# A planned attention and feed-forward kernel: other issue costs for SyncE, second engines only for work due soon, PE's operands taken as ready somewhat later than they end

## The chip, the cores and the metric

The kernel runs on one core of a Trainium2 chip. The core has a matmul engine (PE), a vector engine (DVE), an activation engine (ACT), a general engine (POOL, GpSimd) and SyncE (SP), which issues all DMAs of this kernel; each runs its own list of instructions in order and waits on semaphores. The metric is the time of one launch in device microseconds, the median of several runs.

## The reference

Causal attention over 4 batches, 12 heads, 448 positions and 64 columns a head, then a feed-forward layer pair with an ELU between. Weights come as float64, the rest as float32.

```python
scores = scale * np.matmul(q, k.transpose(0, 1, 3, 2))
scores = np.where(mask, -1000000000.0, scores)          # mask: above the diagonal
scores = scores - np.max(scores, axis=-1, keepdims=True)
attn = np.exp(scores)
attn = attn / (np.sum(attn, axis=-1, keepdims=True) + 1e-09)
x = np.matmul(attn, v)                                  # [B,H,S,D] -> [B*S, H*D] = [1792, 768]
h = x @ w_in                                            # 768 x 2048
g = np.where(h > 0.0, h, np.exp(np.minimum(h, 0.0)) - 1.0)
out = g @ w_out                                         # 2048 x 768
```

## The kernel before

All activations lie transposed, 128 rows of features by 448 columns. A matmul in full precision is made of three in a faster format: each operand is split into a high part (a cast, line 685 on ACT or 686 on DVE) and a low part (the difference, line 688 on DVE or POOL), and `three` (lines 727 to 729) adds high x high, high x low and low x high. Such a **triple** is the unit of PE's main work. Names: `xh`, `xl` are the parts of x, `ph`, `pl` those of a piece of the hidden layer, `whl` both parts of a weight block, `qkhl` those of a block of q and k; `hp` and `op` are the sums of the first and the second layer in PSUM, `G` and `u` hidden values, `w` a weight block.

The weights are converted from float64 on the way (lines 646 to 657: DVE, ACT, DVE, ACT and at last a sum of integers on POOL, `w<-w,w`, which only POOL can do), kept in DRAM and fetched again. In a part of the work one multiplication of blocks in eight is saved by sums and differences of blocks, and these sums (line 693, on DVE or POOL: `G<-G`, `u<-u`, `w<-w` of 384 or 256 columns) are extra work.

Attention goes beside the main matmuls. A group of scores `sc` (line 528) is followed on DVE by the masked copy with its row maximum `nm` (line 335), on ACT by the exponential (339), on PE by transposes `tr` (593), on ACT or DVE by their copy `at` (597), and on PE by the product with the values, `av` (561). Scores and transposes share four PSUM places, the ring `p`: a new tile gets a place when the last reader of the tile that held it is done.

The order of every engine's list comes from a planner, `Plan`. All work is added to it first, each piece with its ways (an engine, a cost in us, the function that writes the instruction), what it reads and writes, and a due time worked back from when PE should do its matmuls. `run` then plays the whole program in a model: of the pieces that could start earliest it takes the one with the earliest due time and writes it to its engine's list. A piece with two ways (casts: ACT, then DVE; differences and sums: DVE, then POOL) goes the second way when that ends it `LEAST` = 0.8 us sooner than waiting for the first, by the model. `port` marks pieces that the model doesn't let run on DVE and POOL at once. A piece is ready `HOP` = 0.22 us after its last operand on another engine; a place of a ring is free as long after its last reader's end (`free_at` in `run`). A load is in place when all earlier ones have been moved, plus `LANDS`.

What the chip does differs from the model where its costs do; the lists stay as they were written.

Of the kernel before, what the change touches and what calls it, by code (L numbers as in the profile page):

```python
# [11 lines left out]
U32 = mybir.dt.uint32  # L12
# [5 lines left out]
CP = 112  # L18
# [90 lines left out]
class Plan:  # L109
# [7 lines left out]

    LANDS = 3.2

    def __init__(self):  # L120
        self.works, self.cap = [], 1e9

# [27 lines left out]
    def run(self):  # L150
        for n, w in enumerate(self.works):
            w.n = n
        for w in reversed(self.works):
            cost = w.ways[0][1]
            lead = 2.0 * cost + 0.4 + (8.0 + 2.0 * w.size if w.size else 0.0)
            dues = [s.due - lead for s in w.succs]
            least = min(dues, default=1e9) - self.AHEAD
            for x in w.bufs:
                if x.ring and not x.ring.in_order:
                    if x.n + x.ring.places < len(x.ring.bufs_of):  # L160
                        dues.append(x.ring.bufs_of[x.n + x.ring.places].due - lead)
                dues += [max(o.due - lead, least if x.ring.long else -1e9) for o in x.after]
            if w.due is None:
                w.due = min([w.cap] + dues)
            for x in w.bufs:
                x.due = min(x.due, w.due)
            w.missing = len(w.preds)
        free, ported = {}, {}
        backlog = {}
        moved = 0.0  # L170
        ready = {w: 0.0 for w in self.works if not w.missing}
        todo = len(self.works)
        self.log = []
        self.done = []
        while todo:
            starts = {}
            for w, t in ready.items():
                skip = {}
                for b in w.bufs:
                    if not b.placed:  # L180
                        f = b.ring.free_at(b, skip.get(b.ring, 0))
                        skip[b.ring] = skip.get(b.ring, 0) + 1
                        if f is None:
                            t = None
                            break
                        t = max(t, f + self.HOP)
                if t is None:
                    continue
                for way, (eng, cost, _, port) in enumerate(w.ways):
                    s = max(t, free.get(eng, 0.0))  # L190
                    if port:
                        s = max([s] + [f for e, f in ported.items() if e != eng])
                    if way:
                        e0, c0 = w.ways[0][:2]
                        before = sum(
                            o.ways[0][1] for o, to in ready.items()
                            if o is not w and o.ways[0][0] == e0 and o.due < w.due and to <= s
                        )
                        if max(t, free.get(e0, 0.0)) + before + c0 < s + cost + self.LEAST:
                            continue  # L200
                    starts.setdefault(eng, []).append((s, w.due, w.n, way, w))
            assert starts, "no work can start"
            eng, cands = min(starts.items(), key=lambda kv: min(kv[1])[0])
            s0 = min(cands)[0]
            s, _, _, way, w = min((c for c in cands if c[0] <= s0 + 0.12), key=lambda c: (c[1], c[2]))
            _, cost, fn, port = w.ways[way]
            if port:
                ported[eng] = s + cost
            for b in w.bufs:
                if not b.placed:  # L210
                    b.placed = True
                    b.ring.order.append(b)
                    b()
            free[eng], w.eng = s + cost, eng
            if w.size:
                moved = max(moved, s + cost) + w.size
                w.end = moved + self.LANDS
            else:
                w.end = s + cost
            self.log.append((s, w.end, eng, w.due, cost))  # L220
            self.done.append(w)
            fn()
            del ready[w]
            todo -= 1
            for b in w.bufs:
                b.left -= 1
                b.end = max(b.end, w.end)
            for o in w.succs:
                o.missing -= 1
                if not o.missing:  # L230
                    o.ready = max(
                        p.end + (0.0 if p.eng == o.ways[0][0] and not p.size else self.HOP) for p in o.preds
                    )
                    ready[o] = o.ready

# [2 lines left out]
def attention_moe_kernel(ctx, tc, qk, v, w_in, w_out, out):  # L238
# [68 lines left out]
    def pool(n, fn, rate=2.3e-3):  # L307
        return ("POOL", 0.1 + rate * n, fn, True)

    def dma(kb, rows, fn, reads, writes, least=0.0, store=False):  # L310
        size = rows * (15.7 + 39.2 * kb / rows) / 16.0e3
        call = (lambda: fn(nc.sync)) if store else fn
        plan.add(("SP", 0.36 if rows <= 128 else 0.57, call, False), reads, writes, size=max(least, size))

# [161 lines left out]
    def loads_23(p, b):  # L478
        n = 2 * CP + S
        raw, hl, t = new("w", [P, n], name="qk"), new("w6", [P, 2, n], F32R, "qkhl"), new("v", [CP, 2, NCH, D])  # L480
        src = qk[b, 2 * p:2 * p + 2].rearrange("h d t s -> (h d) (t s)")[:, 2 * CP:]
        dma(n // 2, P, lambda: nc.sync.dma_start(out=raw(), in_=src), [], [raw])
        dma(224, CP, lambda: nc.sync.dma_start(out=t(), in_=v[b, p]), [], [t])
        hi_lo(lambda: hl()[:, 0], lambda: hl()[:, 1], raw, n, (hl, 0), (hl, 1), raw)
        done(raw)
        return [dict(
            reads=[hl], v=(t, lambda half, x: t()[:, half, x]), split=((0, 0), (0, 1), (1, 0)),
            q=lambda d, i, g=g: hl()[d, i, chunk(g)], k=lambda d, i, n: hl()[d, i, 2 * CP:2 * CP + n],
        ) for g in range(2)]
# [140 lines left out]
    def load64(key):  # L630
        r = words[key] = new("w6", [P, KT, P, 2], U32, "w64")
        if key[0] == "i":
            n, out, src = KT, lambda: r().rearrange("p k c w -> p k (c w)"), w_in[key[1]]
        else:
            x, n = key[2], 4
            out = lambda: r()[:, :n].rearrange("p (h k) c w -> p h k (c w)", h=2)
            src = w_out[key[1]].rearrange("p (h f) c -> p h f c", h=2)[:, :, 2 * x:2 * x + 2]
        dma(n * P, P, lambda: nc.sync.dma_start(out=out(), in_=src.bitcast(U32)), [], [r])

    def convert(key):  # L640
        r, w = words.pop(key), new("w", [P, KT, P])
        n = KT if key[0] == "i" else 4
        size = n * P
        low, high = (lambda: r()[:, :n, :, 0]), (lambda: r()[:, :n, :, 1])
        wf = lambda: w()[:, :n]
        plan.add(dve(size, lambda: nc.vector.tensor_scalar(
            wf(), f32(high()), MOST, -MOST, op0=ALU.min, op1=ALU.max
        ), 0.55e-3, 0.06, True), [(r, 1)], [w])

        plan.add(act(size, lambda: nc.scalar.activation(wf(), wf(), AF.Prelu, scale=REBIAS, alpha=2.0 ** 32), 0.09), [], [w])  # L650
        plan.add(dve(size, lambda: nc.vector.tensor_scalar(  # L651
            wf().bitcast(U32), wf().bitcast(U32), 3, None, op0=ALU.logical_shift_left
        ), 0.55e-3, 0.06, True), [], [w])
        plan.add(act(size, lambda: nc.scalar.activation(
            low().bitcast(I32), low(), AF.Copy, scale=2.0 ** -29
        ), 0.16), [], [(r, 0)])
        plan.add(pool(size, lambda: nc.gpsimd.tensor_tensor(  # L657
            out=wf().bitcast(I32), in0=wf().bitcast(I32), in1=low().bitcast(I32), op=ALU.add
        )), [(r, 0)], [w])
        if key[0] == "i":  # L660
            done(r)
            home, src = kin[key[1]], wf
        else:
            h = key[1] // HALF_E
            home = kout[key[1]].rearrange("p (h f) c -> p h f c", h=2)[:, h:, 2 * key[2]:2 * key[2] + 2]
            src = lambda: wf().rearrange("p (h f) c -> p h f c", h=2)[:, h:]
        k = kept[key] = Buf(None, lambda: home)
        dma(n * 64, P, lambda eng: eng.dma_start(out=home, in_=src()), [w], [k], store=True)
        return w if key[0] == "i" else (w, r)

    def fetch(f):
# [168 lines left out]

    def raw_piece(srcs, reads, dst):
        w = new("w", [P, KT, P])
        dma(KT * 64, 2 * P, lambda: nc.sync.dma_start(out=dst(w()), in_=srcs), reads, [w])
        return in_two(w, KT)

    GROUPS = ((1, 2), (6, 7, 4), (5, 3))
# [265 lines left out]
```

## Time and profile before

| | |
|---|---|
| time, median of 3 runs | 625.55 us (623.75 to 629.59) |
| the profiled execution | 623.13 us, span 621.4 us |
| mean granted clock of PE in it | 0.997 |
| busy of the span | PE 97%, DVE 82%, ACT 69%, POOL 26% |
| chain that ended last, by engine | PE 56%, DVE 15%, ACT 10%, DMA 9%, issue 6% |

The span is the time from the first to the last instruction in one profiled execution; the time of that execution lies 1.7 us above it, and 2.4 us below the median of the runs. Busy time of PE is counted from the start to the end of each matmul, and matmuls overlap, so a busy PE isn't PE at its peak. The chain is followed back from the last instruction to whatever released each one.

### The profile page before, as it was taken

How to read it: one execution, taken by the hardware profiler on the slowest of the kernel's cores; microseconds unless marked ns; L12 is line 12 of the kernel's file. 1: busy time of each engine (PE TensorE's matmuls, PEld its weight loads, DVE VectorE, ACT ScalarE, POOL GpSimd, SP SyncE). 2: the span in 40 equal slices, each digit the busy share in tenths (PEclk: the TensorE clock that was granted, in tenths of full speed). 3: DMA queues.
4: the chain of work that ended last, by engine and by line, in shares of the span. 5: the costliest groups of instructions: out<-in, count | busy, mean ns of one | idle time of the engine just before them, and what ended most of it. 6: DMA issues, size and time to landing. Idle time of an engine off the chain costs nothing.

```text
span 621.4 us, 11699 instructions
## 1 busy us (share of the span) xinstructions
PE 600.4 (97%) x4056; PEld 514.9 (83%) x4056; DVE 508.5 (82%) x1126; ACT 425.9 (69%) x960; POOL 163.2 (26%) x116
## 2 busy tenths in 40 slices
PE   5999999998999999999999999999999999999997
PEld 5655688877788888788788878999999889999996
DVE  4897788689998998989998798597678999998611
ACT  6988889878899989786688684365446765573300
POOL 0235532144343445242220610030001352010000
PEclk9999999998999999999999999999999999999999
DMA  9999999877999999888868598864332343352111
GB/s 218 292 355 360 386 287 271 230 224 247 297 342 344 372 308 300 282 266 261 260 214 268 195 291 243 240 171 127 107 116 84 101 126 104 104 151 69 39 51 45
DMA packets 114172, 135.95 MB, mean 219 GB/s; under 512 B 42560, under 2 KB 86848, under 8 KB 114112
## 3 DMA queue, kind: packets, MB, share of 16 engines
q1 hardware_dynamic: 114112, 135.20, 71.2%
q8 instruction: 32, 0.52, 0.4%
q14 instruction: 28, 0.23, 0.1%
HBM read 103.02 MB, written 32.15 MB: 218 GB/s over the span
## 4 chain that ended last, share of the span: by engine, by line
PE 56%; DVE 15%; ACT 10%; DMA 9%; issue 6%; POOL 2%; SPq 1%; POOLq 0%; DVEq 0%; ACTq 0%
PE op L727 9%; PE op L728 8%; PE op L729 8%; PE hp L727 6%; PE hp L729 5%; PE hp L728 5%; PE hp L749 5%; ACT a L339 4%; PE av L561 3%; PE sc L528 3%; DMA R<-rdram 3%; DMA w<-in_w_out 2%; DVE whl L688 2%; DVE a L335 2%; PE tr L593 2%
## 5 line engine op out<-in xcount | busy, mean ns | idle before, releaser
L685 ACT ACTIVATE whl<-w 128x768 fp32r<-128x768 f32 x90 | 75.6, 842 | 76.8 <-PE op L729 41.4
L727 PE MATMUL op<-ph,whl 128*128 128x448 f32 x336 | 126.6, 377 | 0.0
L728 PE MATMUL op<-pl,whl 128*128 128x448 f32 x336 | 122.8, 365 | 0.0
L729 PE MATMUL op<-ph,whl 128*128 128x448 f32 x336 | 122.7, 365 | 0.0
L688 DVE TENSOR_TENSOR whl<-w,whl 128x768 fp32r<-128x768 f32 x102 | 105.1, 1031 | 20.1 <-ACT whl L685 19.4
L339 ACT ACTIVATE a<-a,nm 112x448 f32<-112x448 f32 (+3 forms) x192 | 97.7, 520 | 28.4 <-DVE nm L335 27.9
L657 POOL TENSOR_TENSOR w<-w,w 128x512 int32<-128x512 int32 (+1 forms) x40 | 67.2, 1683 | 134.7 <-DVE w L651 76.5
L335 DVE CUSTOM_DVE_ANT_0 a<-sc,mask 112x448 f32<-112x448 f32 (+3 forms) x192 | 74.0, 442 | 11.9 <-PE sc L429 7.9
L727 PEld LDWEIGHTS op<-ph,whl 128*128 128x128 f32 x336 | 63.2, 188 | 8.6 <-issue 3.8
L729 PEld LDWEIGHTS op<-ph,whl 128*128 128x128 f32 x336 | 63.1, 188 | 5.1
L728 PEld LDWEIGHTS op<-pl,whl 128*128 128x128 f32 x336 | 63.3, 188 | 4.3
L727 PE MATMUL hp<-ph,whl 128*128 128x448 f32 x168 | 61.7, 367 | 1.4 <-DVE u L815 1.3
L729 PE MATMUL hp<-ph,whl 128*128 128x448 f32 x168 | 61.4, 365 | 0.0
L728 PE MATMUL hp<-pl,whl 128*128 128x448 f32 x168 | 61.3, 365 | 0.0
L597 ACT ACTIVATE at<-tr 112x448 f32<-112x448 f32 (+1 forms) x120 | 53.1, 496 | 5.9 <-PE tr L593 5.9
L727 PE MATMUL hp<-xh,whl 128*128 128x448 f32 x144 | 57.0, 396 | 0.0
L593 PE MATMUL tr<-ident,a 112*112 112x112 f32 x432 | 52.2, 262 | 4.3 <-DVE nm L335 4.3
L593 PEld LDWEIGHTS tr<-ident,a 112*112 112x112 f32 x432 | 45.8, 134 | 12.1 <-DVE nm L335 6.2
L729 PE MATMUL hp<-xh,whl 128*128 128x448 f32 x144 | 53.4, 371 | 0.9 <-DVE whl L688 0.8
L728 PE MATMUL hp<-xl,whl 128*128 128x448 f32 x144 | 53.1, 369 | 0.8 <-DVE xl L688 0.8
L561 PEld LDWEIGHTS av<-at,v 112*64 112x64 f32 x864 | 43.0, 137 | 12.1 <-ACT at L597 5.7
L561 PE MATMUL av<-at,v 112*64 112x112 f32 x864 | 50.9, 264 | 1.1 <-ACT at L597 0.8
(111 smaller groups left out, 1102.2 us busy)
## 6 DMA issues: line engine op xcount, KB each, us to landing
w<-kin SPq DMA_DIRECT2D x44, 384.0 KB, 5.8
w<-in_w_in SPq DMA_DIRECT2D x16, 768.0 KB, 8.3
w<-in_w_out SPq DMA_DIRECT2D x24, 512.0 KB, 6.7
w<-sout SPq DMA_DIRECT2D x32, 384.0 KB, 3.6
w<-kout SPq DMA_DIRECT2D x24, 384.0 KB, 4.5
qk<-in_qk SPq DMA_DIRECT2D x24, 336.0 KB, 5.9
kin<-w SPq DMA_DIRECT2D x16, 384.0 KB, 7.9
sout<-w SPq DMA_DIRECT2D x12, 512.0 KB, 6.9
```

The source lines that it names most:

```text
L335: plan.add(dve(n, lambda: nc.vector.tensor_tensor_reduce(out=a()[:, c], in0=sc()[:, c], in1=mask[:, S - n:], op0=ALU.add, op1=ALU.min, sca ...
L339: plan.add(act(n, lambda: nc.scalar.activation(a()[:, c], a()[:, c], AF.Exp, bias=nm()[:, x:x + 1], scale=-1.0, accum_out=su()[:, x:x + 1] ...
L561: nc.tensor.matmul(av()[half_of(half), chunk(u % 4)], o["v"][1](half, i), at()[:, chunk(x)], start=i == 0, stop=i == chunks(u) - 1,)
L593: nc.tensor.transpose(tr()[:, chunk(x)], a[:, chunk(i)], ident)
L597: act(w, lambda: nc.scalar.activation(at()[:, :w], tr()[:, :w], AF.Copy)),
L657: plan.add(pool(size, lambda: nc.gpsimd.tensor_tensor(out=wf().bitcast(I32), in0=wf().bitcast(I32), in1=low().bitcast(I32), op=ALU.add)), ...
L685: act(n, lambda: nc.scalar.activation(h(), x(), AF.Copy), 0.09),
L688: sub = lambda eng: lambda: eng.tensor_tensor(out=l(), in0=x(), in1=f32(h()), op=ALU.subtract)
L727: nc.tensor.matmul(acc(), wh(k), xh(), start=first, stop=False, skip_group_check=more)
L728: nc.tensor.matmul(acc(), wh(k), xl(), start=False, stop=False, skip_group_check=more)
L729: nc.tensor.matmul(acc(), wl(k), xh(), start=False, stop=last, skip_group_check=more)
L749: pe(ONE, lambda: nc.tensor.matmul(hp(), w[0]()[:, k], x(), start=k == 0, stop=k == KT - 1), [*w, x], [hp], due)
```

## The change

Three rules of the planner are altered; no piece of work is added or removed. A second engine isn't considered for a piece that is due over 20 us after it could start there. A piece of PE counts as ready 0.8 us later than before after its last operand (`START` = 0 lets this hold for all of them); the rule for a ring's places stays. An issue of SyncE costs 0.48 us in the model, or 0.66 for an address with more levels (`long`), instead of 0.36 and 0.57 by the number of rows.

```diff
@@ class Plan @@
     LANDS = 3.2
+
+    SOON = 20.0
+
+    SLACK, START = 0.8, 0.0
@@ Plan.run @@
                     if port:
                         s = max([s] + [f for e, f in ported.items() if e != eng])
+                    if way and w.due > s + self.SOON:
+                        continue
                     if way:
                         e0, c0 = w.ways[0][:2]
...
                     o.ready = max(
-                        p.end + (0.0 if p.eng == o.ways[0][0] and not p.size else self.HOP) for p in o.preds
+                        p.end + (0.0 if p.eng == o.ways[0][0] and not p.size else self.HOP + self.SLACK * (o.ways[0][0] == "PE" and o.due > self.START))
+                        for p in o.preds
                     )
@@ dma and its callers @@
-    def dma(kb, rows, fn, reads, writes, least=0.0, store=False):
+    def dma(kb, rows, fn, reads, writes, least=0.0, store=False, long=None):
         size = rows * (15.7 + 39.2 * kb / rows) / 16.0e3
         call = (lambda: fn(nc.sync)) if store else fn
-        plan.add(("SP", 0.36 if rows <= 128 else 0.57, call, False), reads, writes, size=max(least, size))
+        plan.add(("SP", 0.66 if (rows > P if long is None else long) else 0.48, call, False), reads, writes, size=max(least, size))
...
# long=True: v in loads_23; long=key[0] == "o": load64's load and convert's store; long=False: raw_piece
```

The lists that come out hold the same work. POOL's falls from 64 instructions of lines 688 and 693 to 7, and DVE's casts (line 686) from 45 to 2. The first list is POOL's, around the end of the first attention stage and the start of the second (`w_...<-w_...,w64_...` is the integer sum of a conversion, `pl` and `qkhl` are low parts). Before:

```order
L657 TENSOR_TENSOR w_1552<-w_1552,w64_1377 128x512
L657 TENSOR_TENSOR w_1679<-w_1679,w64_1588 128x512
L688 TENSOR_TENSOR pl_1765<-G_741,ph_1730 128x448
L688 TENSOR_TENSOR pl_1780<-G_745,ph_1756 128x448
L688 TENSOR_TENSOR qkhl_1820<-qk_1708,qkhl_1820 128x672
L657 TENSOR_TENSOR w_1879<-w_1879,w64_1769 128x512
L688 TENSOR_TENSOR pl_1978<-G_757,ph_1888 128x448
L688 TENSOR_TENSOR pl_1993<-G_782,ph_1911 128x448
L657 TENSOR_TENSOR w_1868<-w_1868,w64_1521 128x512
```

and now:

```order
L664 TENSOR_TENSOR w_1678<-w_1678,w64_1563 128x512
L700 TENSOR_TENSOR w64_1563<-w_1401,w64_1563 128x256
L664 TENSOR_TENSOR w_1569<-w_1569,w64_1407 128x512
L695 TENSOR_TENSOR xl_1828<-xs_1787,xh_1815 128x448
L664 TENSOR_TENSOR w_1855<-w_1855,w64_1772 128x512
L664 TENSOR_TENSOR w_1865<-w_1865,w64_1595 128x512
L664 TENSOR_TENSOR w_1970<-w_1970,w64_1825 128x512
```

The `pl` are gone from it, and so is all but one of the `qkhl` in the rest of the list; after its last integer sum POOL has one more instruction, where it had 49.

The second is DVE's, before the softmax of the third group of scores of the second attention stage (ISA is the masked copy with the row maximum). Before:

```order
L686 CAST ph_1911<-G_782 128x448
L822 SCALAR_TENSOR_TENSOR G_1950<-m_1831,hp_1704 128x448
L688 TENSOR_TENSOR whl_1953<-w_1488,whl_1953 128x768
L693 TENSOR_TENSOR w64_1769<-w_1879 128x256
L693 TENSOR_TENSOR w64_1769<-w64_1769,w_1552 128x256
L693 TENSOR_TENSOR w64_1769<-w_1552,w_1879 128x256
L693 TENSOR_TENSOR w64_1769<-w_1552,w64_1769 128x256
L335 ISA a_1918,nm_1920<-sc_1914,mask_71 112x336
```

and now:

```order
L695 TENSOR_TENSOR pl_1888<-G_729,ph_1753 128x448
L700 TENSOR_TENSOR w64_1772<-w_1855 128x256
L700 TENSOR_TENSOR w64_1772<-w64_1772,w_1569 128x256
L700 TENSOR_TENSOR w64_1772<-w_1569,w_1855 128x256
L700 TENSOR_TENSOR w64_1772<-w_1569,w64_1772 128x256
L695 TENSOR_TENSOR whl_1905<-w_1524,whl_1905 128x768
L829 SCALAR_TENSOR_TENSOR G_1967<-m_1833,hp_1695 128x448
L653 TENSOR_SCALAR w_1970<-w64_1825 128x512
L658 TENSOR_SCALAR w_1865<-w_1865 128x512
L695 TENSOR_TENSOR qkhl_1918<-qk_1780,qkhl_1918 128x672
L342 ISA a_1925,nm_1927<-sc_1921,mask_71 112x336
```

The cast has gone to ACT, and DVE makes the `pl` and the `qkhl` itself.

The third is PE's, late in the second attention stage, from a group's last transposes to its values. Before, two triples stand between:

```order
L593 MATMUL tr_4996<-ident_66,a_4753 112x112 x4
L727 MATMUL op_4928<-ph_4722,whl_4658 128x448
L728 MATMUL op_4928<-pl_4729,whl_4658 128x448
L729 MATMUL op_4928<-ph_4722,whl_4658 128x448
L727 MATMUL op_4944<-ph_4699,whl_4658 128x448
L728 MATMUL op_4944<-pl_4720,whl_4658 128x448
L729 MATMUL op_4944<-ph_4699,whl_4658 128x448
L561 MATMUL av_4876<-at_4990,v_4373 64x112
```

and now four, of which the last row and the values behind it are left off here:

```order
L600 MATMUL tr_4987<-ident_66,a_4753 112x112 x4
L734 MATMUL op_4870<-ph_4732,whl_4660 128x448
L735 MATMUL op_4870<-pl_4742,whl_4660 128x448
L736 MATMUL op_4870<-ph_4732,whl_4660 128x448
L734 MATMUL op_4885<-ph_4716,whl_4660 128x448
L735 MATMUL op_4885<-pl_4723,whl_4660 128x448
L736 MATMUL op_4885<-ph_4716,whl_4660 128x448
L734 MATMUL op_4885<-ph_4732,whl_4660 128x448
L735 MATMUL op_4885<-pl_4742,whl_4660 128x448
L736 MATMUL op_4885<-ph_4732,whl_4660 128x448
L734 MATMUL op_4953<-ph_4716,whl_4660 128x448
L735 MATMUL op_4953<-pl_4723,whl_4660 128x448
```

The values moved back by two triples. Between a group's scores and the transposes that follow them stood five or six triples in 19 of 23 groups of this stage and three or four in the others; now there are three to five in 21 of them and six in two.

## Rows read from the trace of the kernel before

**Rows 1.** The page: busy us (share of the span) and number of instructions

```profile
PE 600.4 (97%) x4056; PEld 514.9 (83%) x4056; DVE 508.5 (82%) x1126; ACT 425.9 (69%) x960; POOL 163.2 (26%) x116
```

**Rows 2.** Busy time by stretch: length, each engine (instructions), granted clock, DMA share, GB/s

```profile
404.00:466.00 62.00, 62.00 (x308) 57.48 (x307) 48.05 (x76) 31.33 (x53) 5.77 (x3) 1.00 0.45 130
```

**Rows 3.** Waits of PE: us in total, times, longest us

```profile
PE sc L429 <- DMA k<-in_qk: 5.4, 2, 4.5
PE tr L593 <- DVE nm L335: 4.3, 4, 2.2
...
PE hp L727 <- DVE u L815: 1.3, 1, 1.3
PE hp L728 <- DVE xl L688: 0.8, 1, 0.8
PE av L561 <- ACT at L597: 0.8, 1, 0.8
PE hp L729 <- DVE whl L688: 0.8, 1, 0.8
```

**Rows 4.** Waits of PE's weight loads, the same columns

```profile
PEld av L561 <- ACT at L597: 5.7, 17, 1.0
```

**Rows 5.** Timeline of PE: start us, us, instruction [idle before <- releaser]

```profile
147.55 0.37 PE L729 MATMUL hp<-xh,whl 128*128 128x448 f32 x1
150.15 0.93 PE L593 MATMUL tr<-ident,a 112*112 112x112 f32 x6 [2.24 <-DVE nm L335]
```

**Rows 6.** Timeline of DVE before that transpose

```profile
145.87 1.38 DVE L688 TENSOR_TENSOR whl<-w,whl 128x768 fp32r<-128x768 f32 x1
147.17 1.37 DVE L693 TENSOR_TENSOR w<-w 128x256 f32<-128x256 f32 x1
...
148.91 0.42 DVE L693 TENSOR_TENSOR w<-w 128x256 f32<-128x256 f32 x1
...
149.59 0.50 DVE L335 CUSTOM_DVE_ANT_0 a<-sc,mask 112x336 f32<-112x336 f32 x1
```

**Rows 7.** Timeline of POOL in the same microseconds

```profile
145.13 3.13 POOL L688 TENSOR_TENSOR pl<-G,ph 128x448 fp32r<-128x448 f32 x2
```

**Rows 8.** Timeline of DVE, and of POOL, from 249 us

```profile
249.40 2.06 DVE L688 TENSOR_TENSOR pl<-G,ph 128x448 fp32r<-128x448 f32 x1
251.38 1.50 DVE L693 TENSOR_TENSOR w<-w 128x384 f32<-128x384 f32 x1
...
254.78 0.96 DVE L688 TENSOR_TENSOR whl<-w,whl 128x768 fp32r<-128x768 f32 x1
...
249.02 1.96 POOL L688 TENSOR_TENSOR qkhl<-qk,qkhl 128x672 fp32r<-128x672 f32 x1
250.94 1.52 POOL L693 TENSOR_TENSOR G<-G 128x448 f32<-128x448 f32 x1
```

**Rows 9.** Groups by form: count | busy us, mean ns | idle before, releasers

```profile
L688 DVE TENSOR_TENSOR whl<-w,whl 128x768 fp32r<-128x768 f32 x102 | 105.1, 1031 | 20.1 <-ACT whl L685 19.4
L688 DVE TENSOR_TENSOR pl<-G,ph 128x448 fp32r<-128x448 f32 x54 | 34.9, 662 | 0.6 <-ACT ph L685 0.4
L693 DVE TENSOR_TENSOR w<-w 128x384 f32<-128x384 f32 x25 | 19.1, 765 | 1.9 <-DMA w<-kin 1.4
L686 DVE CAST whl<-w 128x768 fp32r<-128x768 f32 x18 | 10.7, 595 | 7.5 <-PE hp L729 5.4 <-POOL w L657 1.7 <-PE op L729 0.4
...
L685 ACT ACTIVATE whl<-w 128x768 fp32r<-128x768 f32 x90 | 75.6, 842 | 76.8 <-PE op L729 41.4 <-PE hp L729 15.9 <-issue 8.7
```

**Rows 10.** Busy time of two stretches, columns as in 2

```profile
150.00:156.00 6.00, 5.85 (x29) 4.99 (x31) 6.00 (x15) 5.10 (x14) 2.74 (x2) 0.72 0.93 283
124.00:373.00 249.00, 241.91 (x1917) 206.00 (x1916) 229.15 (x515) 203.35 (x474) 92.69 (x63) 0.99 0.88 280
```

**Rows 11.** The page's groups: the integer sums on POOL, columns as in 9

```profile
L657 POOL TENSOR_TENSOR w<-w,w 128x512 int32<-128x512 int32 (+1 forms) x40 | 67.2, 1683 | 134.7 <-DVE w L651 76.5
```

**Rows 12.** Timeline of SyncE's queue

```profile
104.86 1.35 SPq L401 DMA_DIRECT2D R<-rdram  x2
```

More of the change, by code (lines that the diff above doesn't have):

```diff
@@ L482, in loads_23 @@
         dma(n // 2, P, lambda: nc.sync.dma_start(out=raw(), in_=src), [], [raw])
-        dma(224, CP, lambda: nc.sync.dma_start(out=t(), in_=v[b, p]), [], [t])
+        dma(224, CP, lambda: nc.sync.dma_start(out=t(), in_=v[b, p]), [], [t], long=True)
         hi_lo(lambda: hl()[:, 0], lambda: hl()[:, 1], raw, n, (hl, 0), (hl, 1), raw)
@@ L637, in load64 @@
             src = w_out[key[1]].rearrange("p (h f) c -> p h f c", h=2)[:, :, 2 * x:2 * x + 2]
-        dma(n * P, P, lambda: nc.sync.dma_start(out=out(), in_=src.bitcast(U32)), [], [r])
+        dma(n * P, P, lambda: nc.sync.dma_start(out=out(), in_=src.bitcast(U32)), [], [r], long=key[0] == "o")
     def convert(key):
@@ L667, in convert @@
         k = kept[key] = Buf(None, lambda: home)
-        dma(n * 64, P, lambda eng: eng.dma_start(out=home, in_=src()), [w], [k], store=True)
+        dma(n * 64, P, lambda eng: eng.dma_start(out=home, in_=src()), [w], [k], store=True, long=key[0] == "o")
         return w if key[0] == "i" else (w, r)
@@ L842, in raw_piece @@
         w = new("w", [P, KT, P])
-        dma(KT * 64, 2 * P, lambda: nc.sync.dma_start(out=dst(w()), in_=srcs), reads, [w])
+        dma(KT * 64, 2 * P, lambda: nc.sync.dma_start(out=dst(w()), in_=srcs), reads, [w], long=False)
         return in_two(w, KT)
```

## The prediction

> **What bounds the kernel now.** I read the page's busy times first [rows 1]. PE is busy 600.4 of the span's 621.4 us, so any gain has to come out of the 21 us in which it isn't, or out of matmuls that run slower than they need. DVE (82%) and ACT (69%) follow; POOL has 163 us. What one triple of matmuls costs is read where nothing disturbs PE: 308 matmuls in 62 us, 0.201 us each, 0.61 us a triple [rows 2].
>
> Next the waits of PE [rows 3]. The largest, 5.4 us on the first loads of `k`, no plan can shorten by much. Then 4.3 us in four waits of the transposes `tr` for `nm`, the softmax's row maximum on DVE; then single waits for `u` (1.3), `xl` (0.8), `at` (0.8) and `whl` (0.8). The weight loads of PE show the same wait of the values `av` for `at` more often: 17 times, 5.7 us [rows 4], part of it under the matmul still running.
>
> Then why DVE comes late. A transpose's output takes a place of the ring `p`, and those places are held by scores until DVE has read them, so the first row maximum of a group frees the transposes. At 147.55 PE starts a last matmul; the transposes behind it start at 150.15, after 2.24 us of idling that DVE's `nm` ended [rows 5]. In those microseconds DVE ran a `whl` of 1.38 us and a 128x256 `w` of 1.37 us, where the same `w` without company takes 0.42, and only at 149.59 the row maximum [rows 6]. Beside them POOL had two `pl` of 3.13 us together [rows 7]: both are work that the planner had given to POOL as a second engine. It is the same at 249.40, where `pl` takes 2.06 us on DVE and the 128x384 `w` after it 1.50, beside a `qkhl` and a `G` of POOL [rows 8], against means of 0.66 and 0.77 [rows 9]. So an instruction on DVE that meets one on POOL is held up by about a microsecond, and PE pays when a softmax stands behind it.
>
> The Trainium skill says why (SBUF — State Buffer, "SBUF: two separate sides"): the two engines share a pair of ports under an exclusive lock, and a DVE instruction with two SBUF inputs that meets a POOL instruction waits for all of it. The rows agree: the 1.37 us are 0.95 more than 0.42.
>
> The 2.24 us of idling have an aftermath: over 150 to 156 us the granted clock is 0.72 [rows 10], that is 2.4 GHz with a stretch at 1.2 in it. It costs 0.28 x 6 = 1.7 us.
>
> **The change, part by part.** *Second engines only for work due within 20 us.* POOL's list falls from 64 optional instructions to 7; its 40 compulsory ones (`w<-w,w`, 67.2 us [rows 11]) stay. Of the 163 us, 67 are compulsory and some 2 set up constants, so 94 us are optional. DVE receives 57 instructions: 17 `pl` and 24 sums of 448 columns at the mean of `pl`, 0.66, make 27.1 us; 6 `whl` 6.2; 5 `qkhl` at about 0.9, 4.5; 7 sums of 128x384 at 0.77, 5.4; two of 256 columns go the other way, -0.8 [rows 6, 9]. Together 42. DVE gives to ACT 17 casts of `whl` at 0.60 (10.1) and, by their columns, 6 of `qkhl` (3) and 20 of 448 columns (7): 20. Net +22 us for DVE, before any stretch is taken off. ACT takes the 17 at 0.84 (14.3) and the other 26 by their columns (14): 28 us [rows 9].
>
> What of the stretch goes? At 145.87 to 148.5 two DVE instructions lost 0.35 (1.38 against the mean of 1.03) and 0.95, in 3.13 us of POOL: 42%. Of 94 optional us that would be 39 us for the run, the upper end; the lower end is what one group shows by itself, 102 `whl` at a mean of 1.03 against 0.96 undisturbed [rows 8, 9], 7 us. I take about 25, towards the upper end, because the local rows show the collision itself. DVE's total then hardly moves (508 + 22 - 25); what moves is when it is late.
>
> That matters most from 124 to 373 us, where softmax, weights and main matmuls run together: DVE is busy 229 of 249 us, PE idles 7.1 [rows 10]. POOL has 92.7 there; less 21 compulsory ones at 1.68 (35), 57 are optional, 61% of all. DVE so takes up 26 us there, gives up about 8 of casts (40% of 20, the stage's share of the span), and loses between 4 (61% of 7) and 24 (0.42 x 57) of stretch; with 16 it stands at 231.
>
> The four long waits of `tr` should shrink from 4.3 to about 1.0, because at the two whose DVE rows I show an optional instruction of POOL stood beside the lateness: **-3.3** (bounds 0 and -4.3). With the 2.24 us goes the clock's fall: **-1.7** (0 to -1.7). The waits for `u`, `xl` and `whl` (2.9 us together) have DVE as their last engine too, but compulsory POOL work collides as before: half, **-1.5** (0 to -2.9).
>
> *PE's operands taken 0.8 us later than they end.* The planner now puts four triples between the last transposes and the values, where it put two or three: 0.6 to 1.2 us more for the copies `at`. The mean of the 17 waits is 0.34, so the step covers it. PE's own row gives 0.8, its weight loads' 5.7; I take **-2.0**, nearer to the first, since most of a weight load's wait lies under a matmul. This part moves triples about and adds none, so in return the triples between scores and transposes fall from mostly five or six to three to five. The added 0.8 us doesn't guard that place: the freeing of a ring's place is reckoned without it.
>
> *SyncE's issues at 0.48 and 0.66 us* instead of 0.36 and 0.57. In the trace two issues of `R` take 1.35 us, 0.68 each [rows 12], so the new figure is nearer for this form. No wait of PE for a DMA stands in the list except the first, and the first loads stand in the same order: **0** (-1 to +2; a later load of `w` would show first in ACT's and DVE's waits).
>
> New waits: ACT gains 28 us on 426, and the copies `at` are its work; it is at 203 of 249 in the long stage [rows 10]. I set **+1.0** (0 to +5, the size of the present waits for `at`).
>
> Sum: -3.3 - 1.7 - 1.5 - 2.0 + 0 + 1.0 = -7.5 us. The profiled execution took 623.13 us (span 621.4), so 615.6 for its like. The median of the three runs is 625.55, 2.4 above it; against that median the forecast is **618.0 us**. 1% of this kernel is 6.3 us, about what a measurement can tell from no change: the lines are 619.3 and 631.8.
>
> **Rivals.** *DVE becomes the bound and hands the gain back.* In the long stage it takes 26 us and gives up 8: 229 + 18 = 247 of 249 if no stretch vanishes, 243 at the low end of 4. Then every row maximum comes late by whatever has piled up, and the waits for `nm` stay, with fewer but longer collisions against POOL's compulsory work. For it: DVE was full in some stretches already, 6.00 of 6 us from 150 [rows 10]. Against it: the stretch is plain in the rows, and a planner that knows DVE to be busier moves sums with late due times to after 373. Gains left: the values' 2.0 and little else, less ACT's 1.0: 622 to 628, about 624.5.
>
> The Trainium skill has a rule that backs this rival (Perfetto Trace Analysis, "Optimizing Scalar/DVE Operations"): when DVE is saturated, handing some work to ScalarE or even GPSIMD may make sense. The same paragraph warns that the shared port can undo it, which is what the timelines show [rows 6 to 8]; by the rule alone the time would be this rival's 624.5.
>
> *Slower: transposes asked for too early.* With one or two triples fewer behind the scores, DVE has to free the ring's places 0.6 to 1.2 us sooner. At the four places where it was late already (4.3 us in all) each wait grows by that: +2.4 to +4.9; a wait as long as the one of 2.24 costs a fall of the clock at three more of them, 3 x 1.7 = 5.1. With about +7 the time is 632.5. It decides if DVE reaches its row maxima no sooner after the scores than before.
>
> *The change hardly touches what counts:* it does what it says by the order, but waits only change their place, and the time stays at 625.5. I count this with the first rival.
>
> **How the numbers follow.** The forecast gets 0.62, DVE as the bound (with the waits that only move) 0.26, the slower one 0.12. Forecast's own range: with all its terms at their best ends but the values' (-2.0) and no new waits, -4.3 - 1.7 - 2.9 - 2.0 = -10.9, and another -3.7 if the values' waits go in full: 611; at the other end half of the sum, 622. The range takes in the first rival, to 628, and leaves the slower one out: 611 to 628. Of the forecast's 0.62 about 0.52 lie under 619.3; the rest and the first rival are within 1%: 0.36; slower by over 1% is the third: 0.12.
>
> **What would show it.** Right: PE's waits for `nm` under 1.5 us in all, no fall of the granted clock after the start; POOL near 75 us busy; the means of DVE's `whl` and 128x384 `w` down to about 0.96 and 0.6; waits of `av` for `at` a third of 5.7; DVE near 500, ACT near 455. The first rival: DVE over 240 of the 249 us of the long stage, `nm` waits as large as now. The slower one: more than four waits of `tr` for `nm`, each beginning after only three or four triples, and falls of the clock. The forecast would be wrong altogether if PE's idle time lay in waits that the old plan didn't have, on ACT's `at` or on loads.

## The result, and the profile after

The changed kernel took 614.61 us in the median of four runs (613.98 to 619.22), the kernel before 625.83 beside it (623.75 to 629.59): a ratio of 0.9843, with an interval of 0.98 to 0.9886. The profiled execution took 614.32 us where that of before took 623.13, so 8.8 us less; the sum had 7.5.

The page of the changed kernel: span, busy times with shares and numbers of instructions, and the engines in the chain that ended last.

```profile
span 612.5 us, 11705 instructions
...
PE 598.9 (98%) x4056; PEld 513.6 (84%) x4056; DVE 493.1 (81%) x1141; ACT 451.3 (74%) x1002; POOL 76.2 (12%) x59
...
PE 75%; DMA 8%; ACT 7%; DVE 7%; SPq 2%; issue 1%; DVEq 0%; ACTq 0%
```

DVE has 15 instructions more than before and yet 15.4 us less of busy time [rows 1]; its share of the chain has gone from 15% to 7%, and PE's from 56 to 75%. Next the waits of PE and the one of its weight loads for `at` in the changed kernel (us in total, times, longest):

```profile
PE sc L436 <- DMA k<-in_qk: 5.3, 3, 4.5
PE tr L600 <- DVE nm L342: 1.6, 2, 0.9
PE hp L736 <- DVE whl L695: 1.0, 1, 1.0
PE hp L756 <- POOL w L664: 0.9, 1, 0.9
PE tr L600 <- DVE G L829: 0.3, 1, 0.3
...
PEld av L568 <- ACT at L604: 2.8, 9, 0.3
```

This is the whole list of PE. Against [rows 3, 4]: `nm` 4.3 to 1.6, `u` and `xl` gone, `at` gone from PE and halved at the weight loads; `whl` goes from 0.8 to 1.0, and POOL's `w` from 0.2 to 0.9. The windows (length, each engine with its instructions, granted clock, DMA share, GB/s):

```profile
150.00:156.00 6.00, 6.00 (x57) 4.98 (x56) 5.85 (x13) 5.69 (x11) 2.73 (x2) 1.00 1.04 306
124.00:373.00 249.00, 246.03 (x2009) 212.11 (x2010) 232.11 (x549) 216.40 (x499) 39.40 (x28) 1.00 0.92 289
404.00:466.00 62.00, 62.00 (x302) 56.31 (x301) 41.73 (x62) 37.18 (x64) 0.00 (x0) 1.00 0.35 105
```

The clock is whole where it was 0.72, PE does 57 matmuls there instead of 29, and in the same 249 us 92 more [rows 10]. The third row holds something that nobody had asked for: in 62 us without a wait the changed kernel does 302 matmuls, the one before 308 [rows 2]. The end of the document comes back to it.

The groups by form in the changed kernel (count, busy us, mean ns, idle before):

```profile
L695 DVE TENSOR_TENSOR whl<-w,whl 128x768 fp32r<-128x768 f32 x108 | 105.2, 974 | 21.7 <-ACT whl L692 19.8
L695 DVE TENSOR_TENSOR pl<-G,ph 128x448 fp32r<-128x448 f32 x64 | 39.6, 636 | 1.8 <-ACT ph L692 1.8
L700 DVE TENSOR_TENSOR w<-w 128x384 f32<-128x384 f32 x32 | 17.7, 553 | 2.5 <-DMA w<-kin 2.0
```

The timeline of DVE, and of POOL in the last line, at the softmax that answers to [rows 5 to 7]:

```profile
142.33 0.95 DVE L695 TENSOR_TENSOR whl<-w,whl 128x768 fp32r<-128x768 f32 x1
...
144.40 0.85 DVE L695 TENSOR_TENSOR qkhl<-qk,qkhl 128x672 fp32r<-128x672 f32 x1
145.17 0.50 DVE L342 CUSTOM_DVE_ANT_0 a<-sc,mask 112x336 f32<-112x336 f32 x1
...
144.56 1.86 POOL L664 TENSOR_TENSOR w<-w,w 128x512 int32<-128x512 int32 x1 [3.74 <-DVE w L658]
```

DVE's `whl` ahead of this softmax takes 0.95 us where the one of before took 1.38. POOL is idle beside it; its next instruction, beside the `qkhl` and the row maximum, is a compulsory sum. DVE has 64 `pl` of `G` now instead of 54, each 26 ns shorter in the mean. Of the three forms shown, the 384-column sums fall most, from 765 ns to 553 [rows 9].

### The profile page after: what moved, and what is told of

It reads as the page before. It is cut to its first block, busy times and chain, and to the rows that moved or that the text cites. A ratio compares the mean times of both kernels' runs of the same rounds, so it can differ in the third digit from the quotient of the medians.

```text
span 612.5 us, 11705 instructions
## 1 busy us (share of the span) xinstructions
PE 598.9 (98%) x4056; PEld 513.6 (84%) x4056; DVE 493.1 (81%) x1141; ACT 451.3 (74%) x1002; POOL 76.2 (12%) x59
## 4 chain that ended last, share of the span: by engine, by line
PE 75%; DMA 8%; ACT 7%; DVE 7%; SPq 2%; issue 1%; DVEq 0%; ACTq 0%
PE op L734 11%; PE op L735 11%; PE op L736 11%; PE hp L734 7%; PE hp L735 7%; PE hp L736 7%; PE hp L756 6%; PE av L568 5%; PE tr L600 4%; PE sc L535 4%; ACT a L346 2%; DMA sout<-w 2%; DVE a L342 2%; ACT at L604 1%; DMA w<-kin 1%; DMA w<-in_w_in 1%
## 5 line engine op out<-in xcount | busy, mean ns | idle before, releaser
L692 ACT ACTIVATE whl<-w 128x768 fp32r<-128x768 f32 x107 | 90.1, 843 | 65.6 <-PE op L736 40.5
L600 PE MATMUL tr<-ident,a 112*112 112x112 f32 x432 | 50.9, 260 | 2.0 <-DVE nm L342 1.6
L568 PE MATMUL av<-at,v 112*64 112x112 f32 x864 | 48.3, 263 | 0.0
```

Of the source, the lines that this page charges most:

```text
L568: nc.tensor.matmul(av()[half_of(half), chunk(u % 4)], o["v"][1](half, i), at()[:, chunk(x)], start=i == 0, stop=i == chunks(u) - 1,)
L600: nc.tensor.transpose(tr()[:, chunk(x)], a[:, chunk(i)], ident)
L692: act(n, lambda: nc.scalar.activation(h(), x(), AF.Copy), 0.09),
```

## Experiments

All ratios are to the kernel before, run on the same chip. Diffs are against the changed kernel; SyncE's old costs are written "SP old":

```diff
-plan.add(("SP", 0.66 if (rows > P if long is None else long) else 0.48, call, False), ...
+plan.add(("SP", 0.36 if rows <= 128 else 0.57, call, False), ...
```

### Each part alone, and each left out

| kernel | rule for second engines | later readiness | SyncE's new costs | median us | ratio [interval] |
|---|---|---|---|---|---|
| e1_soon | yes | no | no | 618.05 | 0.9885 [0.9847, 0.9923] |
| e2_slack | no | yes | no | 627.9 | 1.0039 [1.0013, 1.0065] |
| e3_sp | no | no | yes | 629.27 | 1.0078 [1.0049, 1.0107] |
| e4_again | yes | yes | yes | 617.83 | 0.987 [0.9839, 0.9901] |
| e5_no_soon | no | yes | yes | 624.77 | 0.9991 [0.9962, 1.0019] |
| e6_no_slack | yes | no | yes | 619.81 | 0.9919 [0.9893, 0.9946] |
| e7_no_sp | yes | yes | no | 617.32 | 0.9867 [0.983, 0.9904] |

**e1_soon**, the rule alone: `SLACK = 0.0`, SP old. 

> The kernel before with the rule on second engines alone (work due over 20 us later stays on its first engine). Theory A (POOL's optional work holds up DVE, and DVE's late row maxima stop PE): most of the gain is here, 617 to 620 us against 625.8, waits of the transposes for the row maximum from 4.3 to under 2 us, no fall of the granted clock after the start, the waits of the values for their copies still near 5 us on the weight loads. Rival B (the later readiness of PE's operands brings the gain): 623 to 627. Rival C (every new plan scatters by some us and this one was lucky): anything from 620 to 632, with waits at other places.

618.05 us: 1.15% faster by itself. POOL falls to 76.7 us busy, DVE to 499.5. No wait for `nm` is left in PE's list; waits for `whl` stand there instead (3.5 us in five). Against the expectation, the granted clock does fall once (0.72 from 184 to 190 us), and the weight loads wait 3.6 us for `at`, not near 5.

**e2_slack**, the later readiness alone: `SOON = 1e9`, SP old. 

> The kernel before with PE's operands taken as ready 0.8 us later, and nothing else. Theory A: the values' waits for their copies fall from 5.7 us on the weight loads to under 3, the waits of the transposes for the row maximum stay at 3 to 6 us since the ring's places aren't guarded: 622 to 625 us. Rival B: 614 to 618. Rival C: 620 to 632.

Slower by 0.4%, where theory A had a small gain. The waits of its PE:

```profile
PE tr L600 <- DVE nm L342: 3.7, 2, 2.1
PE sc L535 <- DVE nm L342: 1.8, 1, 1.8
...
PE hp L734 <- DVE nm L342: 1.5, 1, 1.5
...
PE op L734 <- DVE nm L342: 0.6, 1, 0.6
```

7.6 us for `nm`, where there were 4.3. One of them in the timeline of PE, and then of DVE and of POOL:

```profile
164.50 0.74 PE L600 MATMUL tr<-ident,a 112*112 112x112 f32 x6
166.76 1.14 PE L600 MATMUL tr<-ident,a 112*112 112x112 f32 x8 [1.53 <-DVE nm L342]
```

```profile
163.36 2.80 DVE L700 TENSOR_TENSOR G<-G 128x448 f32<-128x448 f32 x2
166.08 0.61 DVE L342 CUSTOM_DVE_ANT_0 a<-sc,mask 112x448 f32<-112x448 f32 x1
...
162.99 1.63 POOL L664 TENSOR_TENSOR w<-w,w 128x512 int32<-128x512 int32 x1 [0.37 <-DVE w L658]
164.57 2.17 POOL L700 TENSOR_TENSOR w<-w 128x256 f32<-128x256 f32 x2
```

The transposes are asked for while DVE still has two sums of 2.80 us in all, stretched beside POOL, ahead of the next row maximum; POOL's work there is first a compulsory sum, then optional ones. The waits for `at` shrink as this part was meant to do: 1.6 us at the weight loads, in six.

**e3_sp**, SyncE's costs alone: `SLACK = 0.0`, `SOON = 1e9`. 

> The kernel before with the new issue costs of SyncE alone. Theory A: no gain of its own, 623 to 628 us, waits of PE of the same size and kind as before. Rival C: the plan is drawn anew and the time moves by 3 us or more either way although no wait of PE for a load has gone.

Slower by 0.8%, with no wait of PE for a load beyond the first. What grows are waits for `whl` (4.2 us in four) and for `at` (7.8 at the weight loads, 21 times). There are only 0.3 us of waits for `nm`, although POOL has 149.9 us of work, so lateness can come out at `whl` and `at` instead. The time is above theory A's range; it is what rival C had said of a plan drawn anew. No run here tells how the other costs lead to that.

**e4_again**, the changed kernel once more, to see how far two measurements of one program lie apart. 

> The changed kernel once more, unaltered. In its trace the matmuls of the last 235 us start every 206.7 ns, in that of the kernel before every 202.7 ns, without any wait: 4 ns x 1150 matmuls = 4.6 us. If the step is fixed by the program, it is 206.7 again and the time 614 to 615. If it is drawn in each execution, some executions show 202.7 and take about 610 us, or the times fall into two groups 4 to 5 us apart.

No edit. 617.83 us, 3.2 above the first, in ratio 0.3 points; the step between matmuls is 206.7 ns again. So the program fixes the step, but not the time to within the 1 us that was expected with it.

**e5_no_soon**: `SOON = 1e9`. 

> The changed kernel without the rule on second engines (later readiness and SyncE's costs stay). Theory A, as the first runs leave it: POOL's optional work is back, and with it DVE's late row maxima, now met by transposes that stand a triple closer behind the scores: 626 to 632 us, waits of tr for nm of 3 us or more, falls of the granted clock. Rival C (plans scatter whatever the rule): 616 to 632 with no pattern.

The gain is gone, and no more than that: 624.77 us is below theory A's 626 to 632. POOL has 157.2 us again, PE waits 3.4 us for `nm`, 3.3 and 2.7 for `whl`, and the clock is at 0.72 in two windows of 6 us, from 166 and from 230.

**e6_no_slack**: `SLACK = 0.0`. 

> The changed kernel without the later readiness of PE's operands (rule on second engines and SyncE's costs stay). In the run with the rule alone, waits of the triples for whl (3.5 us in five waits, and 1.6 us for ACT's part of it) had come up. Theory A: those stay here, and the waits of the values return to 5 us or more on the weight loads: 618 to 622 us. Rival D (with POOL's optional work gone the 0.8 us have nothing left to cover): 613 to 617.

619.81 us. Waits for `whl` come up (2.8 us on DVE, 2.8 on ACT), and the clock falls twice in the long stage of 124 to 373 us (0.78 from 148 to 154, 0.72 from 228 to 234). The values' waits don't return to 5 us: 3.0 at the weight loads. Beside the two measurements of the whole change that is 0.5 and 0.8 points, and the intervals touch or nearly do.

**e7_no_sp**: SP old. 

> The changed kernel with SyncE's old issue costs. Theory A (the issue costs bring nothing): 613 to 619 us, the same waits as in the changed kernel. Rival E (truer arrival times are needed for the other two to work): 619 to 624, with waits of PE, ACT or DVE for loads.

617.32 us, the whole change's result within its interval: no worth of SyncE's costs shows in this company.

These comparisons hold a term that none of the three parts aims at. After its attention e7_no_sp, like e1_soon, e6_no_slack and e9_pool below, starts its matmuls 4 ns closer together than the changed kernel does (202.7 against 206.7 ns, see the end of the document): over some 1,140 matmuls 4.6 us, or 0.7%. What later readiness and SyncE's costs are worth beside the rule, without this, the table doesn't say. For the rule itself it does: of ten new plans (three of them below), the six with the rule for POOL lie at 0.9843 to 0.9976, the four without it at 0.9991 to 1.0181. Rival C's scatter is real, 1 to 2 points within either group, but the groups don't overlap; e8_place and e5_no_soon lie next to each other.

### The rule for second engines, cut in two

**e9_pool** and **e10_casts**, both with `SLACK = 0.0` and SP old:

```diff
-if way and w.due > s + self.SOON:
+if way and eng == "POOL" and w.due > s + self.SOON:    # e9_pool
+if way and eng != "POOL" and w.due > s + self.SOON:    # e10_casts
```

> The kernel before, with the due-time rule for GpSimd alone: a piece that is not due soon may still go to VectorE as a second engine, but not to GpSimd. Theory A (the gain of the rule is GpSimd's optional work, which stretches VectorE's own): as the rule alone, 617 to 621 us, GpSimd near 75 us busy, VectorE's w<-w,w and pl<-w at their shortest means. Theory B (the gain is VectorE's casts taken back by ScalarE): as before, 623 to 628 us, with GpSimd's work gone and nothing gained.

> The kernel before, with the due-time rule for VectorE as a second engine alone: the early casts go back to ScalarE, GpSimd keeps its optional work. Theory A (GpSimd's optional work is the cost): 623 to 628 us, GpSimd near 150 us busy, VectorE's mean for whl still above 1.02 us. Theory B (VectorE's casts are the cost): 617 to 621 us, waits of TensorE for nm and av gone although GpSimd is as busy as before.

e9_pool took 616.94 us, 0.9876 [0.9849, 0.9904], the gain of the whole rule (e1_soon); e10_casts 635.07, 1.0181 [1.0112, 1.025], so 1.8% slower than the kernel before. The busy times of e9_pool and its windows:

```profile
PE 596.7 (97%) x4056; PEld 514.5 (83%) x4056; DVE 515.1 (84%) x1180; ACT 432.3 (70%) x965; POOL 76.4 (12%) x57
```

```profile
124.00:373.00 249.00, 243.34 (x1972) 208.50 (x1970) 236.87 (x561) 209.49 (x483) 40.09 (x27) 1.00 0.91 286
```

And the busy times, waits and windows of e10_casts:

```profile
PE 612.1 (96%) x4056; PEld 520.8 (81%) x4056; DVE 498.4 (78%) x1082; ACT 451.5 (71%) x1001; POOL 159.4 (25%) x119
```

```profile
PE tr L600 <- DVE nm L342: 6.0, 5, 2.0
...
PEld av L568 <- ACT at L604: 7.4, 22, 1.0
```

```profile
124.00:373.00 249.00, 239.13 (x1871) 201.49 (x1871) 220.20 (x478) 203.36 (x469) 91.28 (x66) 0.98 0.86 269
150.00:156.00 6.00, 4.69 (x41) 3.51 (x38) 5.88 (x14) 5.51 (x11) 2.68 (x3) 1.00 0.64 224
```

Theory A holds: the rule works through POOL. How much of it is DVE's lengthening and how much POOL's own longer pieces (a `pl` of `G` took 1.61 us there in the kernel before, 0.66 on DVE) wasn't tried apart; PE waited for POOL itself only 0.2 us. Of the means that were expected to fall, the 384-column sums' is 552 ns, but that of the 256-column `w<-w,w` stays at 464 ns (457 before). The two kernels also part DVE's load from its lateness. DVE is busier in e9_pool than in any other run here, 515.1 us, and that kernel gains 1.2%; in e10_casts it has 498.4, and the transposes wait 6.0 us for `nm`, more than in any other. What theory A didn't give is the loss of 10 us in e10_casts. Its profiled execution, the longest of four, lost some 10 of its 639.4 us by a mean granted clock of 0.984, against 1.7 us by 0.997 before; its casts ahead of the copies `at` on ACT go with the 22 waits for `at`, but that the casts cause the waits wasn't tried.

### The ring's places

**e8_place** puts the readiness rule's 0.8 us on the freeing of a ring's place as well, for PE's pieces:

```diff
-t = max(t, f + self.HOP)
+t = max(t, f + self.HOP + self.SLACK * (w.ways[0][0] == "PE"))
```

> The changed kernel, and a place of a PSUM ring counts for PE as free 0.8 us later too. Theory A: the remaining waits of the transposes for the row maximum (1.6 us) go, since the plan now leaves 0.8 us behind DVE's reading: 611 to 616 us. Rival: the scores and transposes get their places later, attention is drawn out in the plan, and the time is 616 to 622.

623.58 us, 0.9976 [0.9958, 0.9994]: the expectation was wrong, nearly all of the gain is lost. The wait for `nm` does go (0.6 us), but others come up (POOL's `w` 2.1, `G` 1.9, `xl` 1.2), and the clock falls again, to 0.72 from 142 to 148 us. The rule delays every piece of PE with a ring's place, sums of the main matmuls too, and POOL is given 14 optional pieces instead of 7. What of the two costs the 6 to 9 us (against the two measurements of the changed kernel) isn't told apart.

### The rhythm of the matmuls

**nudge64** puts one matmul of 64 columns ahead of one triple in the last long run of triples (at 400 us), into the sum that this triple then overwrites; the rest of PE's list stays.

```diff
+if (i, r, k) == (1, 0, 0):
+    nc.tensor.matmul(acc()[:, :64], w[1](k), x[0]()[:, :64], start=True, stop=True)
 three(acc, w, k, x, first, last, i in (2, 3))
```

> The changed kernel with one more matmul of 64 columns ahead of the first triple of the second joint block (its sum is overwritten by the triple that follows, so nothing else changes). If the rhythm of the long run of triples is set by where the run starts against some clock of the chip, the run may fall into 202.7 ns in place of 206.7: then 610 to 613 us (some 1100 matmuls by 4 ns less). If the rhythm is set by something else in the program, or by chance of the start: 206.7 ns again and 614 to 618 us, as the changed kernel.

The timeline of PE around it:

```profile
399.62 0.37 PE L734 MATMUL op<-ph,whl 128*128 128x448 f32 x1
399.83 0.37 PE L735 MATMUL op<-pl,whl 128*128 128x448 f32 x1
400.04 0.37 PE L736 MATMUL op<-ph,whl 128*128 128x448 f32 x1
400.24 0.19 PE L931 MATMUL hp<-ph,whl 128*128 128x64 f32 x1
400.27 0.44 PE L734 MATMUL hp<-ph,whl 128*128 128x448 f32 x1
400.55 0.36 PE L735 MATMUL hp<-pl,whl 128*128 128x448 f32 x1
400.75 0.36 PE L736 MATMUL hp<-ph,whl 128*128 128x448 f32 x1
400.95 0.37 PE L734 MATMUL hp<-ph,whl 128*128 128x448 f32 x1
```

Up to the extra matmul the starts lie 206 or 207 ns apart, behind it 202.7 in the mean, to the end of the kernel. The profiled execution took 610.87 us, 3.5 less than that of the changed kernel; some 1,030 matmuls by 4 ns would be 4.1. The median of four runs, 614.38 (ratio 0.9863 [0.9804, 0.9922]), doesn't show it.

**nudge64_again**, the same kernel. 

> The kernel with the extra 64-column matmul, unaltered, a second time. If the rhythm is fixed by the program: 202.7 ns again in the whole run of triples after the last av, a profiled time of 610 to 613 us where the clock does not fall, and a median at or a little below the changed kernel's 614.6. If it is chance at each start: 206.7 ns is as likely, and the median tells nothing from the changed kernel's.

The rhythm falls at the same matmul again, at 408.66 us this time, from 206.7 to 202.7. The median of six runs is 615.96, 0.9839 [0.9801, 0.9876]: against the changed kernel still no difference that can be measured. The runs go from 611.87 to 619.31 us, and the profiled one, the longest, has 4.0 us of waits for `nm` and a clock of 0.997 in it. So what the extra matmul gives in each execution is smaller than what single waits do from one execution to the next.

## Why the prediction was right

618.0 was forecast and 614.6 measured (617.8 the second time), inside the range, and the mechanism is the one named. That the sum of -7.5 came so near the 8.8 us of the profiled execution is in part luck: two terms that it didn't have nearly cancel, as is shown below. Of its signs, the waits for `nm` (1.6 us where under 1.5 was asked) and those for `at` (half of 5.7 where a third was) were missed, the first narrowly. By its steps:

- *Transposes waiting for `nm`, -3.3:* 4.3 to 1.6, so -2.7. e1_soon has no such wait, e5_no_soon has 3.4 us of it, e9_pool none at the transposes and e10_casts 6.0: it is POOL's optional work. (e3_sp, with 0.3 us, shows that not every plan with that work has the wait.)
- *The clock, -1.7:* no fall in the profiled execution until PE has done its last matmul.
- *`u`, `xl`, `whl`, -1.5:* 2.9 to 1.0, so -1.9.
- *Values, -2.0:* 0.8 to nothing at PE, 5.7 to 2.8 at its weight loads. The part that was meant for this isn't needed for the most of it: without the later readiness the weight loads wait 3.0 (e6_no_slack) and with the rule alone 3.6. Where later readiness does show is the first attention stage, which the prediction didn't look at: PE waits 1.3 to 3.2 us there for a copy `at` in all six kernels without it (1.3 in the kernel before) and at most 0.4 in all those with it. The waits for `whl`, 5.1 us in e1_soon, 5.6 in e6_no_slack and 1.0 in the changed kernel, point the same way.
- *SyncE, 0:* as in e7_no_sp. Alone (e3_sp) the new costs lose 0.8%, 4.9 us (3.1 to 6.7), more than the bound of +2, and that stays unexplained.
- *New waits, +1.0:* one of 0.9 us (0.2 before), for POOL's `w`; not for ACT's `at`, where it was looked for.
- *DVE's stretch, 25 us:* summed over a trace, each DVE instruction's duration above the first quartile of its form (of all fourteen traces) went from 52.4 us to 20.5, so 32 and not 25; that is most of the reason why DVE's total fell to 493 where 505 (508 + 22 - 25) was reckoned. Of the 52.4, 32.9 lay beside optional instructions of POOL; in the changed kernel 2.4 do. The same sum is 47 to 59 us in the kernels without the rule for POOL and 19 to 34 in those with it, e8_place the highest of these.

At the four places where the transposes waited for `nm` [rows 3], the prediction showed DVE's rows for two, and the one at 249 us is a wait of only 0.18. The other two, of 1.12 us at 306.81 and 0.74 at 358.75, bear it out. DVE and POOL ahead of them in the kernel before:

```profile
303.62 2.59 DVE L693 TENSOR_TENSOR G<-G,t 128x448 f32<-128x448 f32 x2
303.36 1.84 POOL L688 TENSOR_TENSOR qkhl<-qk,qkhl 128x672 fp32r<-128x672 f32 x1 [0.85 <-ACT qkhl L685]
...
352.96 3.62 DVE L693 TENSOR_TENSOR w<-w 128x384 f32<-128x384 f32 x2
356.50 1.76 DVE L688 TENSOR_TENSOR whl<-w,whl 128x768 fp32r<-128x768 f32 x1
...
354.01 2.16 POOL L688 TENSOR_TENSOR whl<-w,whl 128x768 fp32r<-128x768 f32 x1
356.12 1.33 POOL L693 TENSOR_TENSOR w<-w 128x384 f32<-128x384 f32 x1
```

Optional work of POOL stands beside lengthened instructions of DVE at both. Of the two waits that the changed kernel keeps, the longer (0.92 us at 186.25) follows a `pl` of 1.74 us beside compulsory sums of POOL, the other (0.66 at 278.49) a wait of DVE for a load.

Two things were missing, of opposite signs. Start to start of all matmuls, against the usual step of each kind, some 11 us went from waits that the trace names, where the sum's terms without the clock make 5.8; a good part of the rest is the first attention stage, whose waits for `rr` (the reciprocal of the softmax's sums) and for the copy `at` of line 357 the sum passed over. These are the two rows of the kernel before, and none of after answers to them:

```profile
PE rb L449 <- DVE rr L345: 1.3, 3, 0.9
PE av L367 <- ACT at L357: 1.3, 1, 1.3
```

Against this the slower rhythm takes back 4.4 us (4.6 against 0.2 above 202.7 ns a matmul). With 1.6 of the clock and about 1 of small gaps, -11 - 1.6 - 1 + 4.4 = -9 stands against the 8.8 that the profiled execution gained; the parts are good to about 1 us.

**The first rival**, DVE as the bound: DVE stands at 232.1 of 249 us, near the 231 reckoned (which didn't count that more of the work falls in these 249 us now), and nothing is handed back. e9_pool goes against the rival's mechanism: 236.9 us there, 7.7 more than before, and the gain stays. The Trainium skill (Perfetto Trace Analysis, "Optimizing Scalar/DVE Operations") has both sentences, that a saturated DVE may hand work to GPSIMD and that this might not help, since the two share a port; here the second decided: in e9_pool 87 us of work went from POOL while DVE stood at 82%, for a gain of 1.2%.

**The slower rival**, transposes asked for too early, is real, though not in the changed kernel: e2_slack is this mechanism by itself, with 7.6 us of waits for `nm` and 0.4% lost, 2.4 us, where +7 us had been its price. With the rule beside it `nm` is at 1.6; that this is because DVE reaches its row maxima sooner fits the timelines and isn't shown apart. That guarding the ring's places would mend the rest fell with e8_place.

## What to carry to other kernels

Before a second engine is given work, look at the form means of the first while both run: where they lie well above the undisturbed duration, work that isn't urgent may be cheaper on the first engine, as it was here with DVE over 80% busy. Ask of each instruction ahead of a row maximum (or whatever frees the next buffer) how late it can make that, not how much it adds to the total. Try the parts of a planner's change alone and left out: two of the three here cost 0.4 and 0.8% alone and no harm of theirs beside the third could be measured. And expect each new plan to move the time by some tenths of a per cent, up or down, by waits and rhythms that the change doesn't aim at.

## What the runs showed that was not expected

The same matmul of 448 columns with a new weight block each time runs in one of two steady rhythms at the same granted clock of 1.00 and with no wait in the trace. The timeline of PE in the kernel before, and then in the changed one:

```profile
420.10 0.37 PE L729 MATMUL hp<-ph,whl 128*128 128x448 f32 x1
420.31 0.36 PE L727 MATMUL hp<-ph,whl 128*128 128x448 f32 x1
420.51 0.36 PE L728 MATMUL hp<-pl,whl 128*128 128x448 f32 x1
```

```profile
420.01 0.37 PE L736 MATMUL hp<-ph,whl 128*128 128x448 f32 x1
420.22 0.37 PE L734 MATMUL hp<-ph,whl 128*128 128x448 f32 x1
420.43 0.37 PE L735 MATMUL hp<-pl,whl 128*128 128x448 f32 x1
```

Over hundreds of matmuls the means are 202.7 ns (a pattern of about 199, 207, 202, 203, 202) and 206.5 to 206.7 ns (206, 207, 207). The kernel before, e1_soon, e3_sp, e6_no_slack, e7_no_sp and e9_pool have the first in the whole run of triples after the last `av`; the changed kernel, e4_again and e8_place the second; e2_slack and e5_no_soon go from the second to the first at 511 and 505 us, at two steps lengthened by up to 0.1 us, e10_casts from the first to the second at 520 us, at a wait of 1.3 us for `u`. The kernel before and e3_sp have the same wait at 503.7 and 508.5 us and keep the first. Both kernels that ran twice did the same twice, and one matmul of 64 columns changed it without any pause. So the rhythm isn't chance from one execution to the next: it goes with the program, it lasts for hundreds of matmuls, and a delay can change it but need not. It is worth 4 ns in 207, 2% of such a stretch. What sets it at the start of a run, and whether other short matmuls would switch it the same way, stays open.
